# A two-layer decode step: the reciprocal deviation by a power on GpSimd, merged remainder loads, and a new order table

## The chip, the cores and the metric

The kernel runs on one core of a Trainium2 chip. The metric is the device time of one execution in microseconds. The core has five instruction queues of interest: TensorE (PE in the profile), VectorE (DVE), ScalarE (ACT), GpSimd (POOL), and SyncE (SP), which here does nothing but issue transfers. Every transfer goes through one queue that is served by 16 DMA engines.

## The reference

A decode step of one position for 8 samples, width D = 448, in bfloat16. An attention A and an MLP B are applied, and then the same two again, with the same weights and the same cache:

```
A(x): q = x @ wq -> 16 heads of 256;  k, v = last 1024 of 4096 cached positions, 8 heads, each for 2 query heads
      softmax(q k / 16) v, joined, @ wo          (wq 448x4096, wo 4096x448)
B(x): silu(x @ w1) @ w2                          (w1 448x1792, w2 1792x448)
x = x + A(layernorm(x));  x = x + B(layernorm(x));  x = x + A(layernorm(x));  x = x + B(layernorm(x))
```

The layernorm is (x - mean) / sqrt(var + 1e-5) without weights, so each needs one reciprocal deviation per sample.

## The kernel before

**Data.** The weights are loaded once and stay in SBUF. D = 448 is three blocks of 128 rows and a rest of 64. The three blocks of wq are tiles of 128 x 4096. The rest's 64 rows of 4096 columns are folded so that columns 0 to 2047 lie on partitions 0 to 63 and columns 2048 to 4095 on partitions 64 to 127, a tile of 128 x 2048. w1 is held in the same way (three tiles of 128 x 1792, a rest of 128 x 896). K and V of a sample, 8.39 MB in all, are read once and used by both layers. They go through a ring of 30 slots of 512 KB; each head's K or V fills a slot by two transfers of 256 KB (L713 for K, L719 for V). A transfer is issued when its slot is free and when the transfer ten before it has landed.

**Stages.** Per sample and layer: K is transposed on DVE (L1246, called KT below), PE forms the scores (L881; `S0` for the first layer, `S1` for the second), DVE and ACT do the softmax, PE turns the probabilities (L918, `pT`), ACT copies them to SBUF (L927), PE sums them with ones (L931, `l0`, `l1`) and multiplies them with V (L951, `PV0`, `PV1`). Rows of wo (L1002, `wor`) give the attention's output. The mean and the variance come from matmuls of ones (L1036, L1040, `s12`), with `m2` on ACT and `va` after it. w1's product is L842, its turn to columns L851 on DVE, the normalised value `vt` L1063, then tanh on ACT (L1071), `zh` and `hT` on DVE (L1072, L1074), and w2's rows on PE (L1002 again, `w2r`). The second layer's q comes from L1104 (wq), a turn on DVE (L1109), a selecting matmul (L1115, `qsel`), a subtraction (L1121) and a product that spreads it (L1129, `qbd`, on DVE for one half and on POOL for the other). Sample b's second layer runs between the stages of sample b+1's first layer. The second layer's wo and MLP are done for all eight samples together at the end (`final`).

**The reciprocal deviation** (`rsqrt`, L747). An integer step on the bits (L749) gives a guess, and two Newton rounds improve it. For the MLP's layernorm of a steady sample that is five DVE instructions (L749, L754, L760, L754, L760); for the second layer's attention nine POOL instructions (L749, then L757, L758, L763, L765 twice), after a `va` on ACT (L1051). For the eight samples together, at the start and in `final`, it is seven DVE instructions of 128 x 8.

**Order.** The program is first listed as tasks with reads and writes. SP issues transfers in the listed order: x, wq, K and V of sample 0, wo, w1, w2, then K and V of samples 1 to 7. For the other engines a planner (`schedule`, `tails`) simulates the tasks with modelled durations, ranks them with the offsets of a table, sets the order, and a list of moves then shifts single tasks. The planner also puts in fill matmuls (L1290, 128 x 512, multiplied by zeros) where it sees PE idle for long. Each engine runs its list strictly in order and waits on semaphores where a task needs another engine's result.

Of the kernel before, what the change touches and what calls it, by code (L numbers as in the profile page):

```python
# [1 line left out]

# [12 lines left out]
SEM_LAT = {"pe": 0.05, "dve": 0.05, "act": 0.05, "pool": 0.08, "sp": 0.1}  # L15
LAT = {"pe": 0.17, "dve": 0.07, "act": 0.09, "pool": 0.08, "sp": 0.0}
SWITCH = 0.1
FETCH = (128, 1.4, 0.26)
WINDOW, WARM, ACTIVE, PACED = 3.413, 43.0, 3072.0, 50.0
FIRST, LANDED = 1.2, 1.5  # L20
HOLDS = (("PVc0", 1, "oTc0", 1), ("s12", 1, "hT", 1), ("wq", 2, "qbd", 1))
HELD = ("KT", "max0")
OFFSETS = (
# [26 lines left out]
)  # L50
LOOKS = (0.3, 0.15)

MOVES = {
# [9 lines left out]
    "dve":  # L63
# [6 lines left out]
    "act":  # L70
# [4 lines left out]
    "pool":  # L75
        "",
}
# [14 lines left out]
class Plan:  # L92
# [47 lines left out]
    def tails(self, stay=0.3):  # L140
# [3 lines left out]
        for t in tasks:  # L144
            for i, (o, raw) in t.deps.items():
                succ[i].append((t, raw))
# [1182 lines left out]
```

## Time and profile before

| what | value |
|---|---|
| median of 3 runs | 241.08 us (241.06 to 241.41) |
| profiled execution, span from first to last instruction | 239.7 us |
| busy: PE, DVE, ACT, POOL | 194.1 (81%), 152.8 (64%), 86.5 (36%), 26.0 (11%) us |
| fill matmuls (L1290) | 129, 38.6 us |
| K transposes (L1246) | 128, 81.4 us, 684 ns each |
| read from HBM | 77.67 MB, 324 GB/s over the span |
| issue to landing, wq's blocks, wq's halves, w1's halves | 6.8, 10.2, 11.4 us (median) |

The span leaves 1.38 us of the median outside, around the profiled instructions. A row of the timeline gives the start, the busy time, the engine, the line and the tiles; brackets hold the idle time ahead of it and what ended it. A row of windows gives a stretch of time, the busy time and count of each engine, the granted TensorE clock, the mean busy share of the 16 DMA engines and the rate. The page counts the packets of the queue by size; a transfer's completion is marked by packets of 4 bytes, which are the ones under 512 B. A chain of waits lists what ended last, step by step. Durations on POOL are rough.

### The profile page before, as it was taken

What the parts mean: (1) busy time and instruction counts of PE and PEld (TensorE: products, weight loads), DVE (VectorE), ACT (ScalarE), POOL (GpSimd) and SP (SyncE); (2) the same over time, 40 slices, a digit from 0 to 9 for tenths busy, and PEclk for the clock granted to TensorE, in tenths of its full rate; (3) what the DMA queues carried; (4) which work ended last, traced back from release to release, by engine and by line L of the source; (5) the groups of instructions that cost most, each with busy time, mean ns of one, the idle gap of its engine ahead of it and who ended that gap; (6) DMA issues with size and microseconds to landing.
All of it is one profiled execution on the core that took longest, in us unless ns stands there. A gap on an engine that the chain in (4) does not pass through costs nothing.

```text
span 239.7 us, 8472 instructions
## 1 busy us (share of the span) xinstructions
PE 194.1 (81%) x3567; PEld 97.3 (41%) x3567; DVE 152.8 (64%) x425; ACT 86.5 (36%) x292; POOL 26.0 (11%) x125
## 2 busy tenths in 40 slices
PE   1052358878989899989898898989898999899894
PEld 1051123232345344535433453454344535445552
DVE  7339620037955995996599669946985996334533
ACT  2001231033045516532734354355416440544331
POOL 6100000002010031004001200310031003003000
PEclk9999985999999999999999999999999999999999
DMA  6999999999999999999999999999999999200000
GB/s 228 373 355 403 404 402 384 378 374 406 402 405 403 403 402 404 398 350 379 360 400 402 371 373 379 376 368 377 358 399 399 397 330 399 102 3 3 4 3 1
DMA packets 40341, 78.22 MB, mean 326 GB/s; under 512 B 4320, under 2 KB 6512, under 8 KB 39792
## 3 DMA queue, kind: packets, MB, share of 16 engines
q1 hardware_dynamic: 40304, 77.69, 87.2%
q8 instruction: 28, 0.46, 0.7%
q14 instruction: 9, 0.07, 0.1%
HBM read 77.67 MB, written 0.01 MB: 324 GB/s over the span
## 4 chain that ended last, share of the span: by engine, by line
PE 47%; DMA 19%; DVE 16%; ACT 7%; SPq 7%; issue 4%; POOL 0%; DVEq 0%; ACTq 0%
DMA ring<-in_A_k_cache_dram 10%; PE bank L951 9%; PE bank L881 7%; DMA w2o<-in_B_w_dram 6%; DVE ring L1246 6%; PE bank L1002 6%; PE bank L1290 5%; PE bank L1104 5%; PE bank L1115 3%; DMA ring<-in_A_v_cache_dram 3%; SPq L682 3%; ACT qT L912 2%; DVE mrow L892 2%; PE bank L918 2%; PE bank L958 1%
## 5 line engine op out<-in xcount | busy, mean ns | idle before, releaser
L1246 DVE STREAM_TRANSPOSE ring<-ring 128x512 uint32<-128x512 uint32 x128 | 81.4, 684 | 10.7 <-DMA ring<-in_A_k_cache_dram 10.7
L1290 PE MATMUL bank<-wq_sb,smalls 128*128 128x512 bf16 x129 | 38.6, 386 | 0.0
L881 PE MATMUL bank<-ring,qbd 128*16 128x512 bf16 (+2 forms) x768 | 35.8, 324 | 3.4 <-DVE ring L1246 2.3
L951 PE MATMUL bank<-ring,pT_sb 128*4 128x512 bf16 (+1 forms) x512 | 36.2, 378 | 0.1
L881 PEld LDWEIGHTS bank<-ring,qbd 128*16 128x16 bf16 (+1 forms) x768 | 19.6, 91 | 17.1 <-DVE qbd L1129 3.9
L858 ACT ACTIVATE qbd<-q1s 32x128 bf16<-32x128 bf16 x32 | 10.2, 320 | 42.9 <-PE bank L881 42.3
L892 DVE TENSOR_REDUCE mrow<-bank 128x2 f32<-128x512 f32 (+1 forms) x17 | 11.0, 646 | 11.9 <-PE bank L881 11.1
L1104 PE MATMUL bank<-wq_sb,xn 128*4 128x512 bf16 (+1 forms) x272 | 17.7, 369 | 0.9 <-ACT x2s L1091 0.5
L1018 ACT ACTIVATE qT<-bank 128x448 bf16<-128x448 f32 x16 | 8.7, 543 | 22.4 <-PE bank L1002 22.4
L951 PEld LDWEIGHTS bank<-ring,pT_sb 128*4 128x4 bf16 (+1 forms) x512 | 11.5, 84 | 11.1 <-issue 1.8
L1290 PEld LDWEIGHTS bank<-wq_sb,smalls 128*128 128x128 bf16 x129 | 10.2, 98 | 12.3 <-issue 7.6
L918 PE MATMUL bank<-ident,qT 128*64 128x16 bf16 x256 | 8.5, 180 | 7.3 <-ACT qT L912 6.6
L1002 PE MATMUL bank<-w2o,oT 128*1 128x448 bf16 x224 | 13.2, 352 | 0.7 <-DMA w2o<-in_A_wo_dram 0.7
L956 ACT ACTIVATE qT<-bank 128x512 bf16<-128x512 f32 x16 | 9.6, 597 | 9.7 <-PE bank L951 6.7
L1109 DVE STREAM_TRANSPOSE qT<-bank 128x512 f32<-128x512 f32 (+1 forms) x17 | 11.3, 664 | 2.2 <-PE bank L1104 2.0
L918 PEld LDWEIGHTS bank<-ident,qT 128*64 128x64 bf16 x256 | 6.1, 111 | 12.5 <-ACT qT L912 11.5
L956 ACT ACTIVATE qbd<-bank 128x512 bf16<-128x512 f32 (+1 forms) x16 | 9.1, 570 | 5.5 <-PE bank L951 3.3
L749 POOL TENSOR_SCALAR smalls<-smalls 128x1 int32<-128x1 int32 x8 | 1.5, 190 | 86.9 <-ACT smalls L1051 76.3
L1257 POOL MEMSET qT<- 128x64 bf16 x8 | 1.2, 152 | 82.5 <-PE bank L958 68.7
L1115 PE MATMUL bank<-qT,w2o 128*32 128x64 f32 x128 | 8.4, 352 | 2.0 <-DVE qT L1109 0.8
L912 ACT ACTIVATE qT<-bank,mrow 128x256 bf16<-128x256 f32 x17 | 7.2, 470 | 7.6 <-DVE mrow L905 7.3
L1046 DVE SCALAR_TENSOR_TENSOR smalls<-bank,smalls 128x1 f32<-128x1 f32 x8 | 1.1, 143 | 13.2 <-ACT smalls L1044 9.5
(183 smaller groups left out, 254.6 us busy)
## 6 DMA issues: line engine op xcount, KB each, us to landing
ring<-in_A_k_cache_dram SPq DMA_DIRECT2D x128, 256.0 KB, 6.2
ring<-in_A_v_cache_dram SPq DMA_DIRECT2D x128, 256.0 KB, 6.1
w2o<-in_A_wo_dram SPq DMA_DIRECT2D x2, 1792.0 KB, 13.1
wq_sb<-in_A_wq_dram SPq DMA_DIRECT2D x3, 1024.0 KB, 6.8
w2o<-in_B_w_dram SPq DMA_DIRECT2D x1, 1568.0 KB, 14.5
w_sb<-in_B_w_dram SPq DMA_DIRECT2D x3, 448.0 KB, 12.2
wq_sb<-in_A_wq_dram SPq DMA_DIRECT2D x2, 256.0 KB, 10.2
w_sb<-in_B_w_dram SPq DMA_DIRECT2D x2, 112.0 KB, 11.4
```

Source lines behind the costliest of these rows:

```text
L881: fns.append(lambda e, cb=cb, par=par, j=j, kv=kv, m=m, c0=c0, c1=c1: e.matmul(bank[sc][32 * j:32 * j + m, c0:c1], qbd[layer][:, j * 8 + c ...
L892: dve(lambda e: e.tensor_reduce(mseg[layer][:, ks[0]:ks[-1] + 1], bank[sc][:, lo:hi].rearrange("p (k n) -> p k n", k=len(ks)), AX.X, ALU.m ...
L912: act(lambda e, k2=k2: e.activation(e_sb[ei][:, k2, :, :].rearrange("p uh (jj ul) -> p uh jj ul", ul=2), bank[sc][:, k2 * 256:(k2 + 1) * 2 ...
L918: pe([lambda e, uh=uh, ql=ql, k2=k2: e.matmul(bank[lb][64 * ql:64 * ql + 64, k2 * 64:k2 * 64 + 64].rearrange("p (j q u r) -> p u j q r", j ...
L951: fns.append(lambda e, qh=qh, uh=uh, j=j, vv=vv: e.matmul(bank[ob][32 * j:32 * j + 2 * w, 0:w * DH], p_col(ei, k2, j, qh, uh, w), vv, star ...
L956: act(lambda e: e.activation(o_sb[oi][:, 0:w * DH], bank[ob][:, 0:w * DH], ACTF.Copy), bk(ob), O_K[oi], 0.2 + w * 0.2, "oevh" if ob == OB[ ...
L1002: pe([lambda e, i=i, c=c: e.matmul(bank[XB][32 * c:32 * c + 1, 0:D], rhs(i), w_sb[:, i * D:(i + 1) * D], start=(first and i - i0 < 4), sto ...
L1104: fns.append(lambda e, j=j, c=c, wb=wb, off=off, h0=h0, n=n, k2=k2: e.matmul(bank[wb][32 * j:32 * j + 4, h0:h0 + n], xn[:, part(c, k2), j, :],
L1109: dve(lambda e, wb=wb, h0=h0, n=n: e.transpose(qT[:, h0:h0 + n].rearrange("p (c a i) -> p c a i", a=2, i=32), bank[wb][:, h0:h0 + n].rearr ...
L1115: pe([lambda e, qs=qs, j=j: e.matmul(qs[32 * j:32 * j + 32].rearrange("p (k c r) -> p k r c", k=4, c=8), irep, qT[:].rearrange("p (r c i) ...
L1246: dve(lambda e, v=v: e.transpose(v, v), [("slot", s, h)], [("slot", s, h)], 0.67, "KT")
L1290: fills = {n: [lambda e, j=j, m=P // n: e.matmul(bank[OB[0]][m * j:m * j + m, 0:2 * DH], zero_b.broadcast_to([P, m]), wq_sb[:, 0:2 * DH], ...
```

## The change

**Transfers.** The rest of wq, two transfers of 64 x 2048 to the two halves of the partitions, becomes one, and so does the rest of w1. The one instruction reads the same rows with the column half as the outermost dimension (2 x 64 x 2048 for wq) and writes all 128 partitions. Nothing else moves in SP's order. On SP, the first transfers before:

```order
L669 DMA ring<-in_A_x_dram 8x448
L673 DMA wq_sb<-in_A_wq_dram 128x4096 x3
L676 DMA wq_sb<-in_A_wq_dram 64x2048 x2
L713 DMA ring<-in_A_k_cache_dram 128x1024 x16
L719 DMA ring<-in_A_v_cache_dram 128x1024 x16
L690 DMA w2o<-in_A_wo_dram 128x8x896 x2
L682 DMA w_sb<-in_B_w_dram 128x1792 x3
L685 DMA w_sb<-in_B_w_dram 64x896 x2
L696 DMA w2o<-in_B_w_dram 128x6272
```

and now:

```order
L449 DMA ring<-in_A_x_dram 8x448
L453 DMA wq_sb<-in_A_wq_dram 128x4096 x3
L455 DMA wq_sb<-in_A_wq_dram 128x1x2048
L490 DMA ring<-in_A_k_cache_dram 128x1024 x16
L496 DMA ring<-in_A_v_cache_dram 128x1024 x16
L467 DMA w2o<-in_A_wo_dram 128x8x896 x2
L460 DMA w_sb<-in_B_w_dram 128x1792 x3
L462 DMA w_sb<-in_B_w_dram 128x1x896
L473 DMA w2o<-in_B_w_dram 128x6272
```

The rows show the written side. The third and the eighth have become one transfer each; both stand ahead of K of sample 1.

**The reciprocal deviation** is one POOL instruction, an elementwise power of the variance to a column that holds -0.5 (L525 now), for all three kinds. The bit guess, the Newton rounds, their constants and the scale and sign that went with them are gone. `va` of the second layer's attention moves from ACT to DVE (L811 now). On DVE in a steady sample, from the last K transposes ahead of `va` to `hT`, before:

```order
L1046 SCALAR_TENSOR_TENSOR smalls<-bank,smalls 128x1
L749 TENSOR_SCALAR smalls<-smalls 128x1
L754 SCALAR_TENSOR_TENSOR smalls<-smalls 128x1
L760 SCALAR_TENSOR_TENSOR smalls<-smalls 128x1
L851 STREAM_TRANSPOSE qT<-bank 128x2x224
L754 SCALAR_TENSOR_TENSOR smalls<-smalls 128x1
L1063 SCALAR_TENSOR_TENSOR vt<-cs,smalls,qT 128x14
L760 SCALAR_TENSOR_TENSOR smalls<-smalls 128x1
```

and now:

```order
L1006 STREAM_TRANSPOSE ring<-ring 128x512 x4
L806 SCALAR_TENSOR_TENSOR smalls<-bank,smalls 128x1
L611 STREAM_TRANSPOSE qT<-bank 128x2x224
L823 SCALAR_TENSOR_TENSOR vt<-cs,smalls,qT 128x14
L696 RECIPROCAL rl_sb<-bank 128x16
L832 TENSOR_SCALAR zh<-vt,smalls 128x14
```

The turn of w1's row (L851, now L611) follows `va` directly.

**Order.** The planner, its tables and its moves are gone. A table gives, for each engine, the numbers of the tasks in the order in which it runs them, with marks for fills. 129 fill matmuls become 29, in eleven groups. Many tasks change places. In sample 0, KTs of the fifth and sixth K transfers stand ahead of a copy that q1 (L741) needs. In the steady samples `va` of the second layer and a KT stand on DVE between the turn of q and the subtraction; on PE the residual matmul (L997, now L757) leaves the gap ahead of `qsel`. On PE around the probabilities of sample 3, before:

```order
L1290 MATMUL bank<-wq_sb,smalls 128x512 x2
L918 MATMUL bank<-ident,qT 64x8x2 x16
L1290 MATMUL bank<-wq_sb,smalls 128x512
L931 MATMUL bank<-pT_sb,smalls 128x16 x8
L951 MATMUL bank<-ring,pT_sb 4x512 x28
L958 MATMUL bank<-ident,qT 128x8 x4
```

and now:

```order
L757 MATMUL bank<-xb,ident 128x64
L678 MATMUL bank<-ident,qT 64x8x2 x16
L711 MATMUL bank<-ring,pT_sb 4x512 x22
L691 MATMUL bank<-pT_sb,smalls 128x16 x8
L745 MATMUL bank<-pT_sb,ring 128x32 x16
L718 MATMUL bank<-ident,qT 128x8 x4
```

The sums of the probabilities (L931, now L691) have gone behind 22 of the 28 products with V (L951, now L711).

The diff, cut to what is spoken of:

```diff
+ORDER = {
     "pe":
+        "49 62 56 69 75 96-99 106-107 121-122 111 123 109 112-115 72 124 117 130 119 126 120 129 133-134 138 143-147 "
...
     "dve":
+        "12-13 8 11 4 7 50 3 52 84 5 85 16-17 6 51 82 87 54-55 80 15 88 9 81 63 83 86 89 67-68 57 90 58 93 59 10 14 94 "
...
+    pool(lambda e: e.memset(mhalf, -0.5), [], ["mhalf"], 0.1)
...
         for c in range(3):
             dma(lambda e, c=c: e.dma_start(wq_sb[:, c * HD:(c + 1) * HD], A_wq[c * P:(c + 1) * P, :]),
                 [("wq", c)], P * HD * 2, "wq%d" % c)
-        for h in range(2):
-            dma(lambda e, h=h: e.dma_start(wq_sb[64 * h:64 * h + 64, 3 * HD:],
-                                           A_wq[3 * P:D, h * (HD // 2):(h + 1) * (HD // 2)]),
-                [("wq", 3 + h)], D3 * HD, "wq%d" % (3 + h), rate=220e3)
+        dma(lambda e: e.dma_start(wq_sb[:, 3 * HD:], A_wq[3 * P:D, :].rearrange("r (h n) -> h r n", h=2)),
+            [("wq", 3)], D3 * HD * 2, "wq3")
...
-        for h in range(2):
-            dma(lambda e, h=h: e.dma_start(w1_sb[64 * h:64 * h + 64, 3 * F:], B_w1[3 * P:D, h * F0:h * F0 + F0]),
-                [("w1", 3 + h)], D3 * F0 * 2, "w1%d" % (3 + h))
+        dma(lambda e: e.dma_start(w1_sb[:, 3 * F:], B_w1[3 * P:D, :].rearrange("r (h n) -> h r n", h=2)),
+            [("w1", 3)], D3 * F * 2, "w13")
...
+    def rsqrt(v, y, vk, key, hold):
+        pool(lambda e: e.tensor_tensor(y, v, mhalf.broadcast_to([P, v.shape[1]]), ALU.pow), [vk, "mhalf"] + hold, [key],
+             0.2, "pow")
...
-            act(lambda e: e.activation(va, t2, ACTF.Identity, bias=m2[:, 0:1], scale=-kk / D), bk(bi) + ["m2"],
-                [("va", si)], 0.26, "va")
-        rsqrt(dve if si == 0 else pool, va, rstd, nt, ("va", si), ("rstd", si), [])
+            dve(lambda e: e.scalar_tensor_tensor(out=va, in0=t2, scalar=kk / D, in1=m2, op0=ALU.mult,
+                                                 op1=ALU.subtract), bk(bi) + ["m2"], [("va", si)], 0.16, "va")
+        rsqrt(va, rstd, ("va", si), ("rstd", si), [])
...
-    pl.best_schedule(fill)
+    pl.arrange(ORDER, fills, "oevh")
```

More of the change, by code (lines that the diff above doesn't have):

```diff
@@ L196, in best_schedule @@
-    def best_schedule(self, filler):
-        self.schedule(filler, look=LOOKS[0])
-        tails = self.tails()
-        self.schedule(filler, {t.idx: tails[t.idx] + OFFSETS[max(0, t.batch - 5)].get(t.name.split(".")[0], 0.0)
-                               for t in self.tasks if t.idx in tails}, look=LOOKS[1])
-        for e, moves in MOVES.items():
-            by_idx = {t.idx: t for t in self.order[e]}
-            for pair in moves.split():
-                i, before = (int(x) for x in pair.split(":"))
-                self.order[e].remove(by_idx[i])
-                self.order[e].insert(self.order[e].index(by_idx[before]) if before >= 0 else len(by_idx), by_idx[i])
@@ new lines, in arrange @@
+    def arrange(self, table, fills, reader):
+        work = [t for t in self.tasks if t.eng != "sp"]
+        loads = [t for t in self.tasks if t.eng == "sp"]
+        self.order = {e: [] for e in ("pe", "dve", "act", "pool")}
+        reads = {}
+        for t in self.tasks:
+            if t.name == reader:
+                reads.update((o.idx, t) for o, _ in t.deps.values() if o.name.startswith("PV0"))
+        for e in self.order:
+            last = None
+            for word in table[e].split():
+                if word[0] == "f":
+                    n, _, after = word[1:].partition("@")
+                    t = Task("pe", fills[int(n)], 0.2, 0.0, "fill")
+                    t.idx, t.sem, t.shape = len(self.tasks), None, (512, int(n))
+                    zero = self.last_w["zero_b"]
+                    t.deps[zero.idx] = (zero, True)
+                    if last:
+                        t.deps[last.idx] = (last, False)
+                    if after:
+                        t.deps[loads[int(after)].idx] = (loads[int(after)], True)
+                    self.tasks.append(t)
+                    self.order[e].append(t)
+                    continue
+                lo, _, hi = word.partition("-")
+                for i in range(int(lo), int(hi or lo) + 1):
+                    self.order[e].append(work[i])
+                    last = reads.get(work[i].idx, last)
+        self.order["sp"] = loads
+        assert sum(len(o) for o in self.order.values()) == len(self.tasks)
@@ L525, in bass_interleave_layers__sliding_block_cached__dense_activation_silu__decode_kernel @@
     oT2 = sb("oT2", [P, 2, H, NB], BF16)
-    nmeans, vas, rstds, nts = ([smalls[:, 8 + 2 * u + i:9 + 2 * u + i] for i in range(2)] for u in range(4))
+    nmeans, vas, rstds = ([smalls[:, 8 + 2 * u + i:9 + 2 * u + i] for i in range(2)] for u in range(3))
     nmean = nmeans[0]
+    mhalf = smalls[:, 14:15]
     m2 = smalls[:, 16:17]
@@ L556, in bass_interleave_layers__sliding_block_cached__dense_activation_silu__decode_kernel @@
     x3c = tmf32[:, 464:496].rearrange("p (c b) -> p c b", b=NB)
-    m28, va8, nm8, rs8, nt8 = (tmf32[:, 496 + 8 * i:504 + 8 * i] for i in range(5))
+    m28, va8, nm8, rs8 = (tmf32[:, 496 + 8 * i:504 + 8 * i] for i in range(4))
     xb8 = tmf[:, 1072:1112].rearrange("p (c b) -> p c b", b=NB)
@@ L591, in dve @@
     def dve(fn, reads, writes, dur, name=""):
-        add("dve", fn, reads=reads, writes=writes, dur=max(0.06, dur - LAT["dve"]), name=name)
+        add("dve", fn, reads=reads, writes=writes, dur=dur, name=name)
     def act(fn, reads, writes, dur, name=""):
-        add("act", fn, reads=reads, writes=writes, dur=dur - LAT["act"], name=name)
+        add("act", fn, reads=reads, writes=writes, dur=dur, name=name)
     def pool(fn, reads, writes, dur, name=""):
@@ L700, in bass_interleave_layers__sliding_block_cached__dense_activation_silu__decode_kernel @@
     W2_R = ["w2"] + WO_R
-    WQ_R = [("wq", c) for c in range(5)]
-    W1_R = [("w1", c) for c in range(5)]
+    WQ_R = [("wq", c) for c in range(4)]
+    W1_R = [("w1", c) for c in range(4)]
     slot_of = {}
@@ L1188, in final @@
            ["sqh80", "sqh81", "ones_b"] + TFK + EPSC, bk(sa), (NB, 1), "s128")
-        kk = 4.0 * N26
+        kk = 4.0
         act(lambda e: e.activation(m28, t1, ACTF.Square, scale=float(np.sqrt(kk)) / D), bk(sa) + TFK, ["m28"], 0.19, "m2")
-        dve(lambda e: e.scalar_tensor_tensor(out=va8, in0=t2, scalar=-kk / D, in1=m28, op0=ALU.mult, op1=ALU.add),
+        dve(lambda e: e.scalar_tensor_tensor(out=va8, in0=t2, scalar=kk / D, in1=m28, op0=ALU.mult, op1=ALU.subtract),
             bk(sa) + ["m28"] + TFK, ["va8"], 0.17, "va8")
@@ L1196, in final @@
              ["cs1", "nm8"] + TFK, ["t8"], 0.4, "t8")
[L1197 removed]
+        rsqrt(va8, rs8, "va8", "rs8", TFK)
         y8v = y8.rearrange("p h (j i) -> p (h j) i", i=32)[:, :, 0:NB]
@@ L1292, in bass_interleave_layers__sliding_block_cached__dense_activation_silu__decode_kernel @@
         skip_group_check=True, **({"tile_position": (0, m * j)} if m < P else {})) for j in range(n)] for n in (1, 2, 4)}
-    fill = (fills, 0.214, 2 * DH,
-            lambda n: n.startswith("PV0.") and n.endswith(".0"), "oevh")
-    pl.best_schedule(fill)
+    pl.arrange(ORDER, fills, "oevh")
     first = pl.order["pe"][0]
     first.fns = [lambda e: e.matmul(bank[YB][0:32, 0:1], ident[:, 0:32], ident[:, 0:1], start=True, stop=True)] * PAD + first.fns
-    pl.fill = fill
     pl.emit()
```

258 lines of the change are left out of this document (9 added, 249 removed), and 85 rows, old and new, of tables (MOVES, OFFSETS, ORDER).

## The prediction

> **What bounds the kernel now.** I read the page's head and its chain of waits first, then windows of the start and of the steady part, then the chain in order of time, then single rows. The page:
>
> ```profile
> span 239.7 us, 8472 instructions
> PE 47%; DMA 19%; DVE 16%; ACT 7%; SPq 7%; issue 4%; POOL 0%; DVEq 0%; ACTq 0%
> L1290 PE MATMUL bank<-wq_sb,smalls 128*128 128x512 bf16 x129 | 38.6, 386 | 0.0
> ```
>
> PE heads the chain, but with 129 fill matmuls among its busy time, and the share is a mean over two unlike parts. The windows (time, then busy times, granted clock, DMA share, GB/s) divide them:
>
> ```profile
> core 0: us, PE busy (x) PEld busy (x) DVE busy (x) ACT busy (x) POOL busy (x), PEclk, DMA share, GB/s
> 7.00:10.00 3.00, 0.00 (x0) 0.00 (x0) 1.51 (x10) 0.00 (x0) 0.38 (x4) 1.00 1.03 434
> 10.50:13.50 3.00, 0.00 (x0) 0.00 (x0) 0.00 (x0) 0.00 (x0) 0.00 (x0) 1.00 1.02 223
> 14.00:34.00 20.00, 8.95 (x217) 6.03 (x215) 13.13 (x27) 4.55 (x13) 0.00 (x0) 1.00 1.05 403
> 36.00:40.00 4.00, 3.28 (x40) 1.05 (x32) 0.17 (x1) 1.10 (x2) 0.00 (x0) 0.50 1.06 385
> 46.50:48.00 1.50, 1.27 (x22) 0.38 (x20) 0.00 (x0) 0.18 (x1) 0.00 (x0) 1.00 1.16 276
> 54.00:100.00 46.00, 41.87 (x720) 19.58 (x720) 35.42 (x84) 17.32 (x60) 5.22 (x22) 1.00 1.05 403
> 102.00:108.00 6.00, 5.26 (x84) 1.95 (x72) 5.66 (x19) 2.13 (x10) 0.00 (x0) 1.00 0.99 349
> ```
>
> Up to 100 us the sixteen DMA engines are never idle (share 1.0), and they move 403 GB/s, except where the 64-row transfers of wq (10.5 to 13.5) and of w1 (46.5 to 48) go: full share, 223 and 276 GB/s. After 100 us the rate falls to 349: the ring of slots is full, and the engines behind it set the pace. The chain of the start agrees: DMA until w2 has landed.
>
> ```profile
> 4.49 10.33 DMA ring<-in_A_k_cache_dram
> 14.83 7.59 DMA ring<-in_A_k_cache_dram
> 22.45 6.41 DMA ring<-in_A_v_cache_dram
> 39.34 14.52 DMA w2o<-in_B_w_dram
> ```
>
> The hand-over between the two parts is sample 1's first scores (PE rows of the timeline; the DVE row is the nine transposes of K ahead of them):
>
> ```profile
> 60.79 5.44 DVE L1246 STREAM_TRANSPOSE ring<-ring 128x512 uint32<-128x512 uint32 x9
> 66.56 0.61 PE L881 MATMUL bank<-ring,qbd 128*16 128x512 bf16 x8
> 200.65 1.85 PE L881 MATMUL bank<-ring,qbd 128*16 128x512 bf16 x32
> ```
>
> So the span is a sum of three: 66.56 to sample 1's scores, six periods of (200.65 - 66.56) / 6 = 22.35 to sample 7's, and 239.7 - 200.65 = 39.05 after them. The median, 241.08, lies 1.38 above this span. One sample's K and V are 8.39 MB, 20.8 us at 403 GB/s: no period can be shorter for long.
>
> **The merged transfers.** Before, 64 rows of wq go as two halves, each [64 rows, 4 KB]; now one instruction reads [2][64][2048] and writes 128 partitions. All of it turns on how many engines carry that. The trace has one other small-dimension case: x and the output, 8 rows each.
>
> ```profile
> DMA packets 16, 0.01 MB, mean 2 GB/s; under 512 B 8, under 2 KB 16, under 8 KB 16
> out_dram<-ring SPq DMA_DIRECT2D x1, 7.0 KB
> DMA packets 40341, 78.22 MB, mean 326 GB/s; under 512 B 4320, under 2 KB 6512, under 8 KB 39792
> ```
>
> The first two rows are the window of the output's store, the third is the page. The store has 8 data packets of 896 B and 8 tiny ones, one completion mark for each engine that took part: eight engines, not sixteen. The whole program has 4320 tiny ones. The page lists 269 other transfers (256 of K and V, 13 of weights), all with 64 or 128 rows outermost: 269 x 16 + x's 8 + the store's 8 = 4320 exactly. The number of engines thus follows the outermost dimension. With 2 outermost on the reading side, I take two engines.
>
> [...]
>
> Price of wq's rest: the window at 10.5 moved 3.0 x 223 = 669 KB, which takes 1.66 us at 403, so the halves lose 1.34; their 524 KB cost 1.30 + 1.34 = 2.6 us of all queues. On two engines each moves 262 KB at a sixteenth of 403 to 434 GB/s (25.2 to 27.1): 9.7 to 10.4 us, I take 10.0. Later transfers put a sixteenth on these two engines as well and have landed only when that has, so everything behind is late by 10.0 - 2.6 = **7.4** (7.1 to 7.8). w1's rest: 229 KB, 0.57 us at 403 plus 1.5 x (1 - 276/403) = 0.47 lost, 1.04 now; two engines with 115 KB each take 4.2 to 4.6, I take 4.5: **3.4** (3.2 to 3.5) more. The first users of the weights wait for the queue already, q1 for wq and the first rows of wo for wo:
>
> ```profile
> 13.87 0.28 PE L741 MATMUL bank<-xb,wq_sb 128*128 128x9 bf16 x5 [7.07 <-DMA wq_sb<-in_A_wq_dram]
> 45.06 0.36 PE L1002 MATMUL bank<-w2o,oT 128*1 128x448 bf16 x4 [0.66 <-DMA w2o<-in_A_wo_dram]
> ```
>
> Nothing hides this before sample 1's scores: w2 and then K(1), 4.19 MB or 10.4 us, stand behind both in the queue. K(1) lands at about 53.86 + 10.4 = 64.3, and the nine transposes end at 66.2 because DVE is behind, not the queue; of a late landing at most 66.56 - 64.3 less one transpose of 0.6, so 1.7, is swallowed. Sample 1's scores: 66.56 + 10.8 = 77.4, at best 75.7; I take the middle, **76.6**. That the new order of sample 0 has transposes of K ahead of q1's operands costs nothing, since wo's rows wait for wo, far behind K in the queue.
>
> **The reciprocal deviation.** In a steady sample DVE has the five-step chain around the turned w1 row:
>
> ```profile
> 123.92 0.16 DVE L1046 SCALAR_TENSOR_TENSOR smalls<-bank,smalls 128x1 f32<-128x1 f32 x1 [0.17 <-PE bank L842]
> 124.63 0.64 DVE L851 STREAM_TRANSPOSE qT<-bank 128x448 f32<-128x448 f32 x1
> 125.31 0.24 DVE L1063 SCALAR_TENSOR_TENSOR vt<-cs,smalls,qT 128x14 f32<-128x14 f32 x1
> 125.46 0.15 DVE L760 SCALAR_TENSOR_TENSOR smalls<-smalls 128x1 f32<-128x1 f32 x1
> 125.65 0.31 ACT L1071 ACTIVATE th<-vt,smalls 128x14 f32<-128x14 f32 x1 [1.37 <-DVE smalls L760]
> ```
>
> Without it L851 starts about 0.1 sooner, and tanh waits for vt alone, another 0.1: 0.2 per sample. The power itself runs on POOL between 124.1 and vt's end at 125.4, so it is hidden up to 1.3 us. It waits for va, and behind it in POOL's order stand the second half's qbd product and a memset, both wanted only after hT. Its price is not in the trace. Below it is bounded by one small POOL operation, 0.19, above by the whole nine-step POOL chain it replaces:
>
> ```profile
> 218.43 0.19 POOL L749 TENSOR_SCALAR smalls<-smalls 128x1 int32<-128x1 int32 x1 [9.14 <-ACT smalls L1051]
> 220.72 0.19 POOL L765 TENSOR_TENSOR smalls<-smalls 128x1 f32<-128x1 f32 x1
> ```
>
> That is 220.91 - 218.43 = 2.5 us. I take 0.2 to 0.4, near the row it resembles in form. That chain itself was off the path in the steady samples. The last MLP gains more, as 128x8 Newton steps stand ahead of the turned row and again before z8:
>
> ```profile
> 233.40 0.64 DVE L851 STREAM_TRANSPOSE ring<-bank 128x448 f32<-128x448 f32 x1
> 234.21 0.27 DVE L1199 TENSOR_TENSOR ring<-ring 128x112 f32<-128x112 f32 x1
> 234.58 0.17 DVE L760 SCALAR_TENSOR_TENSOR ring<-ring 128x8 f32<-128x8 f32 x1
> 234.78 0.27 DVE L1200 TENSOR_TENSOR ring<-ring 128x112 f32<-128x112 f32 x1
> ```
>
> L851 moves up by 0.2 to the end of its product, L1199 follows it at once, and L1200 no longer waits for L760: 0.6 off the tail, **38.4** (38.2 to 39.05, the last if the power is late).
>
> **The order.** Ahead of PV of a sample PE now puts nothing but the transposed probabilities:
>
> ```profile
> 116.17 0.28 ACT L927 ACTIVATE pT_sb<-bank 128x128 bf16<-128x128 f32 x1 [0.39 <-PE bank L918]
> 116.50 0.37 PE L931 MATMUL bank<-pT_sb,smalls 128*128 128x16 bf16 x8
> 116.80 0.82 PE L951 MATMUL bank<-ring,pT_sb 128*4 128x512 bf16 x12
> ```
>
> L951 could start at 116.50, and L931's sums are wanted only after PV: 0.3 per sample. Near qsel a fill and a residual matmul leave PE's gap (about 0.3), while the second layer's va, now DVE's (0.16 by L1046's row), and a K transpose stand between turning q and using it (about 0.2 late): zero. Most of the 118 fills left out stood in idle PE: zero, unless the clock falls (rival D). The period is 22.35 - 0.2 - 0.3 = **21.85**; between 21.2 (the gains double) and 22.35 (none).
>
> **Sum**, two engines: 76.6 + 6 x 21.85 + 38.4 = 246.1, plus 1.4 around the span: **247.5 us**. Ends: 75.7 + 6 x 21.2 + 38.2 + 1.4 = 242.5 and 77.4 + 6 x 22.35 + 39.05 + 1.4 = 252.
>
> **Rivals.** B, the other side: the hardware cuts the merged transfer over sixteen engines, after its 128 writing partitions. Then the losses of the halves go, 1.34 + 0.47 = 1.8, and 64.75 + 131.1 + 38.4 + 1.4 = **235.7** (232 to 240), faster. For it: wq's halves, with only 64 partitions, had sixteen marks each. Against it: the 8-row store with its eight. It decides as soon as more than about eight engines carry the load (wq's rest in 2.5 us).
>
> C, the lateness is made up: the steady part has rate to spare (349 against 403 after 102 us). For a full recovery the period must come down to the queue's own 20.8: 75.7 + 124.8 + 38.2 + 1.4 = **240.1**. Against it: what must shrink by 1.5 is the work of PE and DVE, and I count only 0.5.
>
> D, the power is dear or the clock falls. At 2.5 us the power puts tanh 1.2 late in each of seven steady samples; from 1.3 up it decides. With the two engines that gives 247.5 + 8 = **256**, with B's spread 244. Fewer fills may do as much: the same 32 score matmuls as at 200.65 took, after an idle PE,
>
> ```profile
> 28.06 3.40 PE L881 MATMUL bank<-ring,qbd 128*16 128x512 bf16 x32 [1.85 <-DVE ring L1246]
> ```
>
> 1.55 more, and the clock shows 0.50 at 36 to 40, where PE had little. Against it: the new order keeps eleven groups of fills, and real matmuls keep PE busy in the rest.
>
> **How the numbers follow.** Two engines, 247.5: 0.52. B: 0.30. C: 0.08. D: 0.10. About 0.5 us, 0.2%, is what a measurement of this kernel can tell from no change. Slower takes nearly all of the first and most of D, 0.58; same gets half of C and crumbs, 0.06; faster B and the rest of C and D, 0.36. The forecast's own range is 242.5 to 252. B holds too much to be left out, so the range on record is 234 to 251: it leaves out the lower part of B and the upper part of D.
>
> **What would show it.** The two-engine step: the window behind wq's third block with a DMA share far below 1 (2 of 16), q1's wait for wq 7 us longer, and the count of tiny packets on the page, 265 x 16 + 2 x 2 + 2 x 8 = 4260. If instead 4288 are counted (267 x 16 + 16) and the rate stays above 400 from 4 to 34 us, B is right. Order: L931's successor behind PV, periods of 21.85. The power: its POOL row below 1.3 us, tanh waiting for vt. Wrong would be the whole forecast if sample 1's scores start before 70 us.

## The result, and the profile after

The changed kernel takes 259.25 us (median of 4 runs, 257.51 to 263.28) beside 241.25 for the kernel before on the same chip; the ratio is 1.0706, 95% interval 1.0639 to 1.0772. The medians, here and below, are of all executions, while the ratios leave out those that took over 1.5% longer than the fastest of their kernel (here 263.28), so that the two can differ. The forecast was 247.5, and 251 was the upper end of the range. The direction was right; the loss, 18.0 us (17.0 by the ratio), is almost three times the 6.4 that was forecast. The profiled execution is the longest of the four (263.28 us, span 261.4); its mean granted clock is 0.923, that of the three others 0.937 to 0.947.

The page of the changed kernel (its head, the granted clock in 40 slices, the packets, the chain, and the row of the power):

```profile
span 261.4 us, 8189 instructions
PEclk9999999886589799999999999995979999799995
DMA packets 40279, 78.20 MB, mean 299 GB/s; under 512 B 4260, under 2 KB 6452, under 8 KB 39732
PE 41%; DMA 22%; DVE 16%; SPq 8%; ACT 6%; issue 5%; POOL 1%; DVEq 0%; ACTq 0%
L525 POOL TENSOR_TENSOR smalls<-smalls 128x1 f32<-128x1 f32 x16 | 8.7, 542 | 85.8 <-DVE smalls L811 48.2
```

4260 completion marks is the number that the prediction gave for two engines. The clock row has dips from 46 us to the end, where the kernel before had one, between 34 and 42 us. Windows of the same kernel, behind wq's third block and in sample 0:

```profile
12.00:22.00 10.00, 0.00 (x0) 0.00 (x0) 0.00 (x0) 0.00 (x0) 0.00 (x0) 1.00 0.65 194
22.00:24.00 2.00, 0.00 (x0) 0.00 (x0) 0.00 (x0) 0.00 (x0) 0.00 (x0) 1.00 0.13 50
62.00:74.00 12.00, 7.24 (x75) 2.23 (x79) 8.52 (x18) 2.71 (x14) 0.55 (x1) 0.50 0.87 304
```

At 22 to 24 us the DMA share is 0.13, that is 2 of 16, and the rate 50 GB/s, 25 for each of two engines. From 12 to 24 us no compute engine does anything. The chain at the start, and the first scores of samples 1 and 7:

```profile
6.37 18.08 DMA ring<-in_A_k_cache_dram
24.46 6.37 DMA ring<-in_A_k_cache_dram
52.99 13.77 DMA ring<-in_A_k_cache_dram
```

```profile
78.45 2.98 PE L641 MATMUL bank<-ring,qbd 128*16 128x512 bf16 x64 [1.38 <-DVE ring L1006]
219.33 2.12 PE L641 MATMUL bank<-ring,qbd 128*16 128x512 bf16 x40
```

The first K transfer has landed at 24.46, not 14.83. The last of the three rows is sample 1's K, from which DVE's transposes lead to the scores. By the prediction's three parts: 78.45 us to sample 1's scores (before 66.56, predicted 76.6); six periods of (219.33 - 78.45) / 6 = 23.48 (22.35, 21.85); and 261.4 - 219.33 = 42.1 behind them (39.05, 38.4). All three parts are longer than predicted, and the last two went the other way. This execution is 4.0 us above the median, so the parts together are that much longer here than in a median run.

### The profile page after: what moved, and what is told of

Its sections match the earlier page's. It is cut to its first block, busy times and chain, and to the rows that moved or that the text cites. A ratio compares the mean times of both kernels' runs of the same rounds, so it can differ in the third digit from the quotient of the medians.

```text
span 261.4 us, 8189 instructions
## 1 busy us (share of the span) xinstructions
PE 176.9 (68%) x3464; PEld 91.5 (35%) x3467; DVE 145.3 (56%) x379; ACT 86.4 (33%) x285; POOL 23.2 (9%) x72
## 2 busy tenths in 40 slices
DMA packets 40279, 78.20 MB, mean 299 GB/s; under 512 B 4260, under 2 KB 6452, under 8 KB 39732
## 4 chain that ended last, share of the span: by engine, by line
PE 41%; DMA 22%; DVE 16%; SPq 8%; ACT 6%; issue 5%; POOL 1%; DVEq 0%; ACTq 0%
DMA ring<-in_A_k_cache_dram 15%; PE bank L711 10%; DMA ring<-in_A_v_cache_dram 7%; DVE ring L1006 7%; PE bank L762 6%; PE bank L641 5%; PE bank L864 5%; PE bank L602 2%; SPq L460 2%; SPq L473 2%; PE bank L875 2%; DVE qT L869 2%; ACT qT L778 2%; ACT qT L672 2%; PE bank L678 2%
## 5 line engine op out<-in xcount | busy, mean ns | idle before, releaser
L1006 DVE STREAM_TRANSPOSE ring<-ring 128x512 uint32<-128x512 uint32 x128 | 82.7, 686 | 25.6 <-DMA ring<-in_A_k_cache_dram 25.6
L711 PE MATMUL bank<-ring,pT_sb 128*4 128x512 bf16 (+1 forms) x512 | 41.5, 399 | 6.4 <-ACT pT_sb L687 2.7
L864 PE MATMUL bank<-wq_sb,xn 128*4 128x512 bf16 (+1 forms) x272 | 20.0, 412 | 1.6 <-ACT xn L846 1.4
L518 PE MATMUL bank<-xb,wq_sb 128*128 128x9 bf16 x128 | 3.6, 168 | 24.7 <-DVE xb L559 24.7
L711 PEld LDWEIGHTS bank<-ring,pT_sb 128*4 128x4 bf16 (+1 forms) x512 | 12.6, 86 | 17.9 <-issue 11.8
L525 POOL TENSOR_TENSOR smalls<-smalls 128x1 f32<-128x1 f32 x16 | 8.7, 542 | 85.8 <-DVE smalls L811 48.2
L762 PE MATMUL bank<-w2o,oT 128*1 128x448 bf16 x224 | 16.1, 386 | 0.1
L696 DVE RECIPROCAL mrow<-bank 128x16 f32<-128x16 f32 x8 | 2.1, 258 | 22.2 <-PE bank L691 22.2
L618 ACT ACTIVATE qbd<-q1s 32x128 bf16<-32x128 bf16 x32 | 10.2, 319 | 11.9 <-PE bank L641 11.3
L602 PE MATMUL bank<-w_sb,xbt 128*1 128x448 bf16 (+1 forms) x128 | 10.0, 378 | 6.0 <-DMA w_sb<-in_B_w_dram 3.8
L869 DVE STREAM_TRANSPOSE qT<-bank 128x512 f32<-128x512 f32 (+1 forms) x17 | 11.3, 664 | 1.7 <-PE bank L864 1.2
L518 PEld LDWEIGHTS bank<-xb,wq_sb 128*128 128x128 bf16 x128 | 3.5, 104 | 24.8 <-DVE xb L559 24.8
```

The source lines that it names most:

```text
L602: pe([lambda e, i=i, k=k, c=c: e.matmul(bank[bi][32 * c:32 * c + n, 0:FN], lhs(k), w1_sb[:, i * F + c * FN:i * F + (c + 1) * FN] if i < 3 else
L711: fns.append(lambda e, qh=qh, uh=uh, j=j, vv=vv: e.matmul(bank[ob][32 * j:32 * j + 2 * w, 0:w * DH], p_col(ei, k2, j, qh, uh, w), vv, star ...
L762: pe([lambda e, i=i, c=c: e.matmul(bank[XB][32 * c:32 * c + 1, 0:D], rhs(i), w_sb[:, i * D:(i + 1) * D], start=(first and i - i0 < 4), sto ...
L864: fns.append(lambda e, j=j, c=c, wb=wb, off=off, h0=h0, n=n, k2=k2: e.matmul(bank[wb][32 * j:32 * j + 4, h0:h0 + n], xn[:, part(c, k2), j, :],
L869: dve(lambda e, wb=wb, h0=h0, n=n: e.transpose(qT[:, h0:h0 + n].rearrange("p (c a i) -> p c a i", a=2, i=32), bank[wb][:, h0:h0 + n].rearr ...
L1006: dve(lambda e, v=v: e.transpose(v, v), [("slot", s, h)], [("slot", s, h)], 0.67, "KT")
```

## The experiments

**Is it the merged load?** In the changed kernel the remainders were put back as two half transfers each, with nothing else touched:

```diff
-        dma(lambda e: e.dma_start(wq_sb[:, 3 * HD:], A_wq[3 * P:D, :].rearrange("r (h n) -> h r n", h=2)),
-            [("wq", 3)], D3 * HD * 2, "wq3")
+        for h in range(2):
+            dma(lambda e, h=h: e.dma_start(wq_sb[64 * h:64 * h + 64, 3 * HD:],
+                                           A_wq[3 * P:D, h * (HD // 2):(h + 1) * (HD // 2)]),
+                [("wq", 3 + h)], D3 * HD, "wq%d" % (3 + h))
...
```

(and w1's in the same way).

> The changed kernel with the two remainder loads put back as two half transfers each; power and order stay. Theory A (the merged load on two engines is the main cause): sample 1's first scores come back from 78.45 to about 66 to 67 us, and the time falls by 11 to 12 us, to about 246 to 248. What is left over the kernel before is then the clock and the order. Theory B (the clock, because fills are gone): the time falls by less than 12 and windows at clock 0.5 stay in the steady samples, about 248 or more. Theory C (the late start itself starves TensorE and so brings the low clock): the low windows go with it, and the time is 236 to 240.

Measured: 247.94 us beside 241.26, ratio 1.0197 (1.0114 to 1.0279). Page and first scores:

```profile
PEclk9999999985899999999999797999999999799995
66.10 2.92 PE L644 MATMUL bank<-ring,qbd 128*16 128x512 bf16 x64 [1.37 <-DVE ring L1009]
204.49 2.06 PE L644 MATMUL bank<-ring,qbd 128*16 128x512 bf16 x40
```

Theory A holds: the change is 11.3 us shorter without the merged load (12.3 by the ratios), and sample 1's scores are back at 66.10. But 6.7 us (4.8 by the ratio) are left over the kernel before, and the dips of the clock stay, as theory B has it for the rest; so theory C falls. The mirror image is the kernel before, in its own order and with its fills, with the merged loads alone. After the planner has set the order, the first half's task issues the whole transfer, and the second's is dropped:

```diff
+    whole = {
+        "wq": lambda e: e.dma_start(wq_sb[:, 3 * HD:], A_wq[3 * P:D, :].rearrange("r (h n) -> h r n", h=2)),
+        "w1": lambda e: e.dma_start(w1_sb[:, 3 * F:], B_w1[3 * P:D, :].rearrange("r (h n) -> h r n", h=2))}
+    for w in ("wq", "w1"):
+        one, two = tw[w + "3"], tw[w + "4"]
+        one.fns = [whole[w]]
+        pl.order["sp"].remove(two)
...
```

> The kernel before, with its own order, fills and Newton steps, and only the two remainder loads merged. Theory A: DMA share near 0.65 and less behind wq's third block, 4260 completion marks, the first scores of sample 1 some 11 us later than 66.56, the time 251 to 253. Theory B (most of the change's loss is the clock and not the load): 244 or less. If the steady part makes up for the lateness: 241 to 243.

Measured: 254.86 us, ratio 1.0573 (1.0527 to 1.062), 13.6 us more, somewhat above theory A's range. The page's packets, and the scores of samples 1 and 7:

```profile
DMA packets 40281, 78.22 MB, mean 309 GB/s; under 512 B 4260, under 2 KB 6452, under 8 KB 39732
80.48 0.61 PE L881 MATMUL bank<-ring,qbd 128*16 128x512 bf16 x8
214.17 1.88 PE L881 MATMUL bank<-ring,qbd 128*16 128x512 bf16 x32
```

The lateness at sample 1, 13.9 us, is carried to the end: the period is (214.17 - 80.48) / 6 = 22.28, as before, and the clock of this execution was 0.993. Nothing is made up, so rival C falls too. Then each of the two loads alone, by the same edit with only one name in its loop:

> The kernel before with only wq's remainder merged. The prediction's term was 7.4 us; the changed kernel's first K transfer landed 24.46 - 14.83 = 9.6 us late. If the two-engine load alone makes it: sample 1's first scores 9.5 to 10 us later than 66.56 and the time 250.5 to 251.5. If the term as predicted holds and the rest of the 13.6 comes from both loads meeting: 248 to 249.

Measured: 250.95 beside 241.53, ratio 1.0385 (1.0348 to 1.0422).

```profile
23.50 3.55 PE L741 MATMUL bank<-xb,wq_sb 128*128 128x9 bf16 x128 [16.70 <-DMA wq_sb<-in_A_wq_dram]
50.70 4.45 PE L1290 MATMUL bank<-wq_sb,smalls 128*128 128x512 bf16 x15 [0.23 <-issue]
76.09 0.61 PE L881 MATMUL bank<-ring,qbd 128*16 128x512 bf16 x8
```

q1 starts 9.6 us later than before (23.50, 13.87 in the prediction's row), and sample 1's scores 9.5 us later. The lateness goes through sample 0's own products: the fills ahead of wo's rows stood in a wait before (the rows behind them still waited 0.66 us for wo), while here the rows wait for the fills alone.

> The kernel before with only w1's remainder merged. The prediction's term was 3.4 us; if the two terms add up to the 13.6 measured with both, about 4: 244.5 to 245.5. If w1's load is hidden behind w2, which only the end of sample 0's first layer needs: 241 to 242.

Measured: 244.36, ratio 1.0152 (1.0077 to 1.0227).

```profile
52.13 0.92 PE L842 MATMUL bank<-w_sb,xbt 128*2 128x448 bf16 x14 [1.86 <-DMA w_sb<-in_B_w_dram]
68.39 0.61 PE L881 MATMUL bank<-ring,qbd 128*16 128x512 bf16 x8
```

Sample 0's product with w1 waits for it until 52.13 (50.14 in the kernel before). At sample 1's scores wq's load costs 9.5 us, w1's 1.8, and both together 13.9, which is 2.6 more than the sum. The same product in the run with both loads, and then in the run with wq's alone, shows where these come from:

```profile
62.81 1.66 PE L842 MATMUL bank<-w_sb,xbt 128*2 128x448 bf16 x14 [3.29 <-DMA w_sb<-in_B_w_dram]
59.83 0.92 PE L842 MATMUL bank<-w_sb,xbt 128*2 128x448 bf16 x14
```

Behind wq's load, w1's makes the product 3.0 us late, not 2.0, and behind the idle 3.29 us the matmuls are slower: 14 take 1.66 us in place of 0.92, and the three fills behind them 1.46 in place of 0.82. That is 3.0 + 1.4 = 4.4 us for w1's load, the 13.9 - 9.5 at the scores.

**What would one transfer over all engines bring?** It is what rival B supposed. The same bytes, with row r's two halves on partitions 2r and 2r + 1, make a transfer with 128 outermost (the products that read these rows are left as they were, so this kernel gives a price and not the layer's result):

```diff
-        "wq": lambda e: e.dma_start(wq_sb[:, 3 * HD:], A_wq[3 * P:D, :].rearrange("r (h n) -> h r n", h=2)),
+        "wq": lambda e: e.dma_start(wq_sb[:, 3 * HD:], A_wq[3 * P:D, :].rearrange("r (h n) -> (r h) n", h=2)),
...
```

> The kernel before with each remainder in one transfer whose outermost dimension is 128: row r's two column halves go to partitions 2r and 2r + 1 (the products that use the remainder are not adapted, so q and the MLP's first product are computed from rest rows in the wrong place; the work and the bytes are the same). It is what rival B supposed: one transfer over sixteen engines. Rival B's price: the halves' losses of 1.34 and 0.47 go, 1.8 us in all, 239.3 to 240 beside 241.3. If transfers are not the limit at the end of the span: 241 to 241.5.

Measured: 240.42 beside 241.57, ratio 0.994 (0.9917 to 0.9964). Windows at the places of the two halves, and the packets:

```profile
10.50:13.50 3.00, 1.17 (x44) 1.20 (x45) 0.00 (x0) 0.00 (x0) 0.00 (x0) 1.00 1.03 401
46.50:48.00 1.50, 0.85 (x20) 0.30 (x13) 0.00 (x0) 0.54 (x1) 0.00 (x0) 1.00 1.03 434
```

```profile
DMA packets 40309, 78.22 MB, mean 328 GB/s; under 512 B 4288, under 2 KB 6480, under 8 KB 39760
```

4288 marks, 401 and 434 GB/s in place of 223 and 276, and 1.15 us gained (1.4 by the ratio) where 1.8 was expected. Merging was worth trying; the outermost dimension of 2 was the fault.

**The fills.** The kernel before with its 129 fill matmuls taken out of PE's finished order:

```diff
+    pl.tasks = [t for t in pl.tasks if t.name != "fill"]
+    pl.order["pe"] = [t for t in pl.order["pe"] if t.name != "fill"]
```

> The kernel before with all 129 fill matmuls left out and everything else in its order. Theory B (fills hold the clock): windows at 0.5 in the steady samples, mean clock near 0.93, 5 to 10 us slower, 246 to 251. Rival (they stand in idle time and do nothing for the time): 240 to 241.5.

Measured: 253.74 beside 241.26, ratio 1.043 (1.0364 to 1.0495): 12.5 us by the medians, 10.4 by the ratio, at or above the upper end of theory B. The clock, two groups of matmuls that took 378 and 369 ns each with fills, and the same 28 products with V in two samples of this run:

```profile
PEclk9999999999878979986989789999979999799998
L951 PE MATMUL bank<-ring,pT_sb 128*4 128x512 bf16 (+1 forms) x512 | 41.0, 415 | 0.5 <-ACT pT_sb L927 0.5
L1104 PE MATMUL bank<-wq_sb,xn 128*4 128x512 bf16 (+1 forms) x272 | 23.5, 466 | 2.3 <-ACT xn L1086 1.1 <-ACT x2s L1091 0.5 <-ACT xn L1087 0.5
74.49 3.52 PE L951 MATMUL bank<-ring,pT_sb 128*4 128x512 bf16 x28
99.31 1.90 PE L951 MATMUL bank<-ring,pT_sb 128*4 128x512 bf16 x28
```

The first of the two, 3.52 us, stands where the clock row has 7 and 8 (slices of 6.3 us, 69.8 to 82.5), the second, 1.90 us, where it has 9. Matmuls that nothing reads are thus worth 10 to 12 us here, because the real ones run at a lower clock behind a quiet stretch: the mean granted clock is 0.93 in this run and 0.986 in the kernel before, and the changed kernel has 0.50 over 62 to 74 us, behind 4 us with 0.28 us of matmuls. Such a stretch need not be one gap: one dip follows an idle time of 4.09 us (63.4 to 67.5), but another, from 87.9 on (16 products of L1104 take 1.61 us there, 1.03 from 137.54 on), follows 3.5 us in which TensorE was busy for 1.74 us and no gap was longer than 0.91. Their return to the changed order, with half transfers, took two attempts. The first put 88 of them in PE's table (`f1` is one fill; a number behind @ is the load that it waits for), 14 of them ahead of sample 0's wo rows, which are task 119:

```diff
-        "49 62 56 69 75 96-99 106-107 121-122 111 123 109 112-115 72 124 117 130 119 126 120 129 133-134 138 143-147 "
+        "49 62 56 69 75 96-99 106-107 121-122 111 123 109 112-115 72 124 117 130 f1 f1 f1 f1 f1 f1 f1 f1 f1 f1 "
+        "f1@38 f1@38 f1@38 f1@38 119 126 120 129 133-134 138 f1@40 f1@40 f1@41 f1@41 f1@42 f1@42 143-147 f1 f1 f1 "
...
```

> The changed kernel with half transfers again and with 88 fills of 128 x 512 at about the places where the kernel before has them (behind w2's rows, behind the fold, ahead of and behind the turned probabilities, in the waits of the start and the end) in place of its own 29. Theory A with B: the clock stays at 1.00 from 60 us on, the period is 21.5 to 22, 236 to 240. If order or power is itself a loss: 242 to 246, at a clock of 1.00.

Measured: 245.4, ratio 1.0133 (1.0055 to 1.0211). That lies in the second range, but not for the second reason; the timeline of PE at sample 0's wo rows (L768) shows where it is lost:

```profile
45.53 3.31 PE L1056 MATMUL bank<-wq_sb,smalls 128*128 128x512 bf16 x14
48.78 0.55 PE L768 MATMUL bank<-w2o,oT 128*1 128x448 bf16 x8
70.35 2.92 PE L647 MATMUL bank<-ring,qbd 128*16 128x512 bf16 x64
```

In the new order PE comes out of sample 0's products with V only when wo has landed. Fills put there are in the way, as are six more that wait for w1 ahead of its product (2.72 us from 52.82), and sample 1's scores start at 70.35. The second attempt adds 61 to the change's own 29 and none at these two places:

```diff
-        "49 62 56 69 75 96-99 106-107 121-122 111 123 109 112-115 72 124 117 130 119 126 120 129 133-134 138 143-147 "
+        "49 62 56 69 75 96-99 106-107 121-122 111 123 109 112-115 72 124 117 130 119 126 120 129 133-134 138 "
+        "143-147 f1 f1 f1 f1 f1 f1 154 f1 156 170-171 162 172-173 175 178-180 f4 181 186-187 183 188-189 f1 f1 "
...
```

> Half transfers, the new order and power, and fills in the steady samples and at the end as in the run before with 88 fills, but at the start only six ahead of sample 0's w2 rows and two ahead of sample 1's scores, so that no fill stands between sample 0's wo rows and the transfer they wait for. If the late start (70.35 instead of 66.10) was the fills' own doing: first scores at 66 to 67, periods of 21.8 at a clock of 1.00, 237.5 to 239.5. If the new order is itself slower: 241 to 243.

Measured: 241.22 beside 241.53 (10 runs), ratio 0.9996 (0.9971 to 1.0021). This kernel has the tasks of the run with half transfers in the same order on PE and differs from it by the fills alone. So 6.7 us of the change (247.94 to 241.22; 4.9 by the ratios) were the missing fills, and what is left of the change, its order and its powers, is no faster than the kernel before. The scores of samples 1 and 7, and the chain of waits around sample 7's first products with V:

```profile
65.39 2.97 PE L647 MATMUL bank<-ring,qbd 128*16 128x512 bf16 x64 [0.84 <-DVE ring L1012]
198.80 2.06 PE L647 MATMUL bank<-ring,qbd 128*16 128x512 bf16 x40
197.21 1.04 PE bank L647 x30
198.27 6.77 DMA ring<-in_A_v_cache_dram
205.17 1.32 PE bank L717 x15
```

Sample 7's scores start 1.85 us before those of the kernel before (200.65), but its products with V only at 205.17, against 205.45 there. The chain goes through V's transfer: its last slots are freed by sample 6's second-layer scores (L647 at 197.21), and from there it takes 6.8 us. In this kernel an earlier sample 7 waits for its own V. Its start is as the first theory had it, but the period is (198.80 - 65.39) / 6 = 22.24, not 21.8, and the mean granted clock 0.976, not 1.00; the part behind sample 7's scores is 42.3 us (39.05 before). Where all of that part's loss comes from was not tried. The same table in the changed kernel, with its merged loads:

> The changed kernel with its merged transfers, and with the fills added as in the run that kept the start (half transfers there, 241.2). If fills and transfers are separate causes that add up: 241.2 plus the 11.3 to 13.6 of the merged load, 252.5 to 254.8. If the clock loss in the changed kernel comes from the late start and more fills do not help it: 257 to 259.

Measured: 255.67, ratio 1.0564 (1.0533 to 1.0596). That is 14.5 us above the run with half transfers, near the 13.6 that the load costs in the order of before. Fills win 6.7 us with half transfers but 3.6 (259.25 - 255.67) with merged ones (4.9 and 3.4 by the ratios), so the causes add up only roughly.

**The power.** In the kernel before, the five DVE steps of each MLP layernorm were replaced by one power on GpSimd, and nothing else but the scale and sign of the variance ahead of it (`g` are the five steps of a sample, `h` the first GpSimd step of its second-layer chain, ahead of which the power is put):

```diff
+        new.eng, new.deps, new.name = "pool", deps, "pow"
+        new.fns = [lambda e: e.tensor_tensor(y, v, mhalf.broadcast_to([P, v.shape[1]]), ALU.pow)]
...
+    for g, h in zip(small, heads):
+        one_pow(g, vas[0], rstds[0], h)
...
```

> The kernel before, its order and fills, with only the five-step DVE chain of the eight MLP layernorms (128 x 1) replaced by one power on GpSimd each. The prediction's term: 0.2 us per sample, 1.2 to 1.6 in all, 239.5 to 240.2. If the last V transfers set the end of the stream whatever happens per sample: 241 to 241.5.

Measured: 240.51 beside 241.57 (10 runs), ratio 0.9956 (0.9931 to 0.9981). A steady sample, and the scores of samples 1 and 7:

```profile
123.25 0.57 POOL L1320 TENSOR_TENSOR smalls<-smalls 128x1 f32<-128x1 f32 x1 [4.06 <-DVE smalls L1046]
124.32 0.24 DVE L1063 SCALAR_TENSOR_TENSOR vt<-cs,smalls,qT 128x14 f32<-128x14 f32 x1
124.59 0.31 ACT L1071 ACTIVATE th<-vt,smalls 128x14 f32<-128x14 f32 x1 [1.22 <-DVE vt L1063]
65.97 0.61 PE L881 MATMUL bank<-ring,qbd 128*16 128x512 bf16 x8
198.84 1.86 PE L881 MATMUL bank<-ring,qbd 128*16 128x512 bf16 x32
```

The power ends at 123.82, half a microsecond ahead of the start of vt; tanh waits for vt. The period is (198.84 - 65.97) / 6 = 22.15, the predicted 0.2 less. Five traces of this order with the five steps have periods of 22.28 to 22.43, and the next run, also with the small powers, 22.09, so the 0.2 is more than what traces differ by. With the next run, this version is the fastest of those that compute the whole: it beats both kernels. Then the last MLP's 128 x 8 as well (`big[1]` are its seven steps, and the power goes to the end of GpSimd's order, behind t8):

```diff
+    one_pow(big[1], va8, rs8, None)
```

> The same, and the last MLP's 128 x 8 reciprocal deviation too by one power in place of seven DVE steps. The prediction's term was a gain of 0.6. By the 1.65 us that the power took in the changed kernel, behind t8 on GpSimd: 1.0 to 1.6 slower than the run without it.

Measured: 240.56, ratio 0.9964 (0.9941 to 0.9986), equal to the run without it within what can be told.

```profile
232.09 1.68 POOL L1320 TENSOR_TENSOR ring<-ring,smalls 128x8 f32<-128x8 f32 x1
233.87 0.27 DVE L1200 TENSOR_TENSOR ring<-ring 128x112 f32<-128x112 f32 x1 [1.01 <-POOL ring L1320]
```

L1200 waits 1.01 us for a power of 1.68. It starts 2.57 us behind va8 (which started at 231.30), where the seven steps let it start after 2.16 (234.78 - 232.62): a loss of 0.4, below the size expected and below what the times can show. The reverse was tried on the changed order with half transfers and fills:

```diff
-        rsqrt(va8, rs8, "va8", "rs8", TFK)
+        newton8(va8, rs8, nt8, "va8", "rs8", TFK)
...
```

> The same, with the last MLP's reciprocal deviation (128 x 8) by seven DVE steps as in the kernel before, ordered as there; the 16 powers of 128 x 1 stay. In the changed kernel the power of 128 x 8 took 1.65 us and the product behind it waited 1.42. Theory: 1.0 to 1.5 us below the run without it. If the tail has another limit at once: equal within 0.5.

Measured: 241.05 (10 runs), ratio 0.9982 (0.9945 to 1.0019), 0.17 below the run with the power: the times cannot tell it apart from nothing.

**The moved sums.** The last term of the prediction, alone, on the order of before with the small powers (`pv` are the eight groups of a sample's products with V, `l0` its sums; samples 1 to 7):

```diff
+            pe_o.remove(l0)
+            pe_o.insert(pe_o.index(pv[5]) + 1, l0)
```

> The kernel before with the eight small powers (240.51 beside 241.57 without) and one term of the new order alone: on TensorE the sums of the probabilities (L931 of the first layer) go behind 22 of the 28 products with V in samples 1 to 7. The prediction's term: 0.3 us per sample, period 22.15 to 21.85, 238.5 to 239.3. If the place of the sums is not on the path: 240.2 to 240.8. If DVE's reciprocal behind them now comes late: 241 or more.

Measured: 241.44 beside 241.32 (12 runs), ratio 0.9993 (0.9972 to 1.0014): the gain of the powers (0.9956) is gone. The scores of samples 1 and 7 and a steady sample with the sums moved, and then that sample's products with the sums in front (the run of the small powers):

```profile
67.77 0.61 PE L881 MATMUL bank<-ring,qbd 128*16 128x512 bf16 x8
201.66 1.83 PE L881 MATMUL bank<-ring,qbd 128*16 128x512 bf16 x32
118.07 1.46 PE L951 MATMUL bank<-ring,pT_sb 128*4 128x512 bf16 x22
119.46 0.36 PE L931 MATMUL bank<-pT_sb,smalls 128*128 128x16 bf16 x8
119.76 0.60 PE L951 MATMUL bank<-ring,pT_sb 128*4 128x512 bf16 x6
```

```profile
115.58 0.36 PE L931 MATMUL bank<-pT_sb,smalls 128*128 128x16 bf16 x8
115.88 1.90 PE L951 MATMUL bank<-ring,pT_sb 128*4 128x512 bf16 x28
```

The products do start at once now, but the sums still stand ahead of the last six of them: 2.29 us from the probabilities to the last product (118.07 to 120.36), 2.20 with the sums in front (115.58 to 117.78). The period is (201.66 - 67.77) / 6 = 22.32, 0.17 longer. This profile is of the longest of the twelve executions (243.14), and its sample 1 starts 1.8 us later (67.77, 65.97) before any moved sum has run, so the start is no effect of the move. The third theory's reason does not show: DVE's reciprocal behind the sums has ended at 120.12, and its reader starts at 120.58, released by PE (L958). That the move gains nothing is thus explained; the rest of the 0.17 is not.

## Why the prediction was right or wrong

- **Two engines: right.** The 8-row store had told it, and the change shows 4260 marks and 2/16 of share (0.13). Rival B fell, but one transfer did go over sixteen engines when 128 was outermost (4288 marks, 401 and 434 GB/s).
- **The lateness: right in kind, too small.** The prediction took 10.0 us at sample 1's scores; the changed kernel is 11.9 late there, and the merged load costs it 11.3 (12.3 by the ratios). wq's term was 7.4, but the first K transfer is 9.6 late in the changed kernel, and so is q1 in the run with wq's load alone: the load holds up the queue for about 9.6 + 2.6 = 12.2 us, not 10.0. The pace was right at the end of the load (25 GB/s for each engine at 22 to 24 us); why the load takes longer than 262 KB at that pace was not tried. w1's term was 3.4; it measured 1.8 alone and 4.4 behind wq's load. The path was right for the changed kernel, whose chain goes through sample 1's K. In the order of before the lateness goes through sample 0's products instead, and of the slack of 1.7 only 0.1 shows there (9.6 to 9.5). That the steady part does not make it up was right: the period with the loads alone is 22.28.
- **"Most of the 118 fills left out stood in idle PE: zero": wrong, and the largest miss.** They stood in idle time, and taking them out cost 6.7 us (4.9 by the ratios) all the same. The count was off too: 129 - 29 = 100 matmuls are gone, and 118 is 129 less eleven, with each of the six groups of four that run side by side counted as one. Their worth is not in the time they fill but in the clock of the matmuls behind them (products with V 378 ns each with fills and 415 without, in the kernel before). The prediction had it in rival D, gave D 0.10, and let eleven groups of fills speak against it; the page after has dips from 46 us to the end. What the profile of before offered was a price, 1.55 us for one slow group of scores, but no count of the gaps that slow matmuls would follow; and over that group (28.0 to 31.5) the granted clock reads 1.00, so the record does not tie this price to the clock. The rows at 0.50 would have: 12 products with V took 1.87 us there (from 37.58), and 28 take 1.90 in a steady sample.
- **The small powers: right.** 0.2 us per sample, hidden on GpSimd; 0.54 to 0.57 us each, a little above the 0.2 to 0.4 taken.
- **The power at the end: wrong.** The step priced 128 x 8 by the row of 128 x 1. It takes 1.64 to 1.68 us, and the product behind it waits: 0.4 lost where 0.6 was to be gained.
- **The moved sums, 0.3 per sample: wrong.** The step looked at the first product ("L951 could start at 116.50"), but the turn of the result (L958) comes behind the last in PE's order, and the sums still stand ahead of that. Alone the move costs 0.17 per sample by one trace, of which 0.09 shows around these products.
- **The sum.** The prediction's own gains, 0.5 per period and 0.65 at the end, 3.65 in all, came out as 0.3 (241.53 - 241.22), with the load's 1.3 too little (11.3 for 10.0) and the fills' 6.7 at nothing. These three make 11.65 of the 11.75 us between 247.5 and 259.25, but they must: each is the difference of two neighbours in a row of runs that leads from the kernel before to the changed one, so that the agreement is no proof. By the other way, over the run with more fills and merged loads, the load's share is 14.5 and that of the fills 3.6, so each share is known to some 3 us.

## What to carry to other kernels

Count the completion marks on the page: they told here how many engines carry a transfer (4260 with 2 outermost, 4288 with 128), and a merged transfer should keep its large dimension outermost (two engines cost 11 to 14 us here, sixteen gained 1.15). A matmul that nothing reads can be dear to remove: before fills are called free, look for the places where TensorE would fall quiet, and price the matmuls right behind them at the clock that the dips of the trace show (0.50 here). When work is moved behind its neighbour in one queue, follow the last instruction of the group, not the first, and look for a transfer that sets the end anyway.

## What the runs showed of the hardware

- A power on GpSimd took 0.54 us for 128 x 1 and 1.64 for 128 x 8 in the changed kernel, so about 0.16 for each further column, an estimate from these two.
- While two engines drained, the other fourteen came to stand idle: with ten transfers in flight the DMA share of the changed kernel is 0.65 over 12 to 22 us and 0.13, that is 2 of 16, over 22 to 24.
- With two halves of 64 partitions in flight the queue moved 223 and 276 GB/s at a full DMA share; in the same windows of the kernel with 128 partitions at a time it moved 401 and 434.
- Without fills the kernel before has dips of the clock from 63 us to the end (a mean of 0.93, 0.986 with them) and is 10 to 12 us slower, though TensorE is then still busy for 71% of it; one dip follows 3.5 us in which TensorE was half busy, without a gap above 0.91 us.
